# Splitting one more block product of a sequence-mixing matrix product, and reordering stores and gates around it

## The chip, the cores and the metric

The kernel runs on one core of one Trainium2 chip. The metric is the device time of one execution in microseconds (us), less is better. The core's engines run side by side, each with its own queue of instructions, in order: TensorE (PE, matrix products into PSUM banks), VectorE (DVE), ScalarE (ACT), GpSimd (POOL), and SyncE (SP), which here only issues DMAs.

## The reference

Two layers of two blocks each, on x of 2048 rows (S) by 512 columns (D), all in fp32:

```
x = x + A(layernorm(x))     # linear attention, 32 heads of 16
x = x + B(layernorm(x))     # gated MLP with mixing along the sequence
# and both once more

def B(x, w_in, w_sp, b_sp, w_out):
    z  = gelu(x @ w_in)                 # 2048 x 1792
    z1 = z[:, :896]
    z2 = layernorm(z[:, 896:])
    g  = w_sp @ z2 + b_sp[:, None]      # 2048 x 2048 times 2048 x 896: the mixing
    return (z1 * g) @ w_out
```

The weights are the same in both layers. The change concerns the mixing of layer two above all.

## The kernel before, in words

**Three products for one.** Every fp32 operand is split into a high part (ACT copies it to the format fp32r) and a low part (DVE subtracts the high part from the original). One fp32 product is then three matmuls: high x high, high x low, low x high. `high` (L222) and `low` (L225) are the helpers; the mixing has its own (L1777 and L1780 for blocks of w_sp, 128x1024; L1840, L1842 and L1844 for z2).

**Seven block products.** The mixing is cut into 2 x 2 blocks and done as seven block products instead of eight, with sums of blocks as operands (class `P4`; P1 to P7 in the order of `ORDER`: P2, P1, P6, P7, P4, P5, P3). The sums of w_sp's blocks (`Sums`) are made once, in layer one, kept in DRAM, and loaded again in layer two. The sums of z2's blocks are made in place in SBUF when a product needs them (`zsp`, operations on columns named H1, H2 and H3; "the H2 operations" are the subtraction and the addition that prepare columns H2). Products share PSUM banks: P6 goes on accumulating in P1's banks, and P7 in P6's.

**Two kinds of product.** An undivided product runs in eight steps along the contracted dimension: 24 matmuls of 128x512 a step where its `WITH3` columns are needed (P1, P2, P4, P5), 18 for the others (P6, P7, P3). A divided one (`DIVIDED`) is split into seven again, of half depth: fourteen steps of 12 matmuls (`mm_div`; the order of the seven is `SEVEN`, r = 1, 5, 6, 2, 7, 3, 4, two steps each, q = 0 and 1). Its operands are sums of quarter blocks of w_sp, which lie in DRAM (`halves`: a copy of one part, then an accumulating DMA from POOL's queue adds the other; `halve` does one of these each time it is called, from a list `parts`). After each pair of steps DVE adds the bank's content into units of the result (`evac_div`; a unit is 128 columns of the result over 512 rows, `unit(n, f)` in an SBUF tile `gb[n]`, called bg in the profile). Where the next product accumulates on, some columns are carried over into a bank by ACT (`carry`).

Before the change, layer one divides P2 and P4, layer two P2, P4 and P5.

**What a step needs.** Two steps ahead, `sp` prepares: the block of w_sp is loaded by SP (five steps ahead), ACT makes its high part, DVE its low part; for an undivided step DVE makes the sum of z2's blocks, ACT its high part, DVE its low part. `KEPT` products store their low parts of w_sp in layer one and load them in layer two by a DMA from POOL's queue (L1783), so that DVE doesn't make them again.

**Gates.** A finished unit is multiplied by z1, which comes from DRAM (`ask` loads up to three units of z1 ahead, in the order of `gates()`). One gate runs per step (`tick` of `P4`); those of P1's units on POOL (L2043), tied behind the latest high part of w_sp on ACT (`self.mark`). `evac` empties the banks of the undivided products on DVE (L2057 after P1, L2060 after P6).

**The rest.** Behind the mixing `out7` does the product with w_out and, in layer one, prepares layer two's attention. The order of all instructions is written out by hand: each engine's queue is what the code issues, in that order. The sums for the mixing are made in layer one beside the attention and the first product of block B: `Sums.tick` stores the last sums, fetches raw blocks and adds two of them on POOL. All pages (SBUF tiles of 128x512, `pg` in the profile) come from one pool of 22 and go round: a page that is put back is the next one's, as soon as the DMA that reads it has ended.

Of the kernel before, what the change touches and what calls it, by code (L numbers as in the profile page):

```python
# [15 lines left out]
P = 128  # L16
# [79 lines left out]
DIVIDED = ("P2", "P4"), ("P2", "P4", "P5")  # L96
KEPT = ("P7", "P5")
# [63 lines left out]
def mixer_kernel(ctx: ExitStack, tc: tile.TileContext, x_in, wqkv, wo_d, win1_d, win2_d, wsp_d, bsp_d, wout_d,  # L161
# [300 lines left out]
    class P1:  # L462
# [370 lines left out]
    class P2:  # L833
# [498 lines left out]
        def run(self, sums):  # L1332
# [4 lines left out]
            for s in range(1, NT + 3):  # L1337
# [3 lines left out]
                if s < 5:  # L1341
# [100 lines left out]
        def odd(self, s, p, q, r):  # L1442
# [168 lines left out]
    class Sums:  # L1611
# [3 lines left out]
        def __init__(self):  # L1615
# [13 lines left out]
            self.parts = [(what, p, m, q) for p in ("P4", "P5")[:len(DIVIDED[1]) - 1] for what in ("copy", "add") for m in (1, 3, 2, 4)  # L1629
                          for q in range(2)]  # L1630

# [6 lines left out]
        def halve(self, n, after, i=None):  # L1638
# [4 lines left out]
            row = 2 if p == "P2" else 0  # L1643
            j, s = {1: ((1, 0), (1, 4)), 3: ((0, 0), (1, 0)), 2: ((0, 0), None), 4: ((0, 4), None)}[m][what == "add"] or (0, 0)
            src = self.s1[j, s + 2 * q:s + 2 * q + 2] if p == "P5" else wsp_d[row + j, HT + s + 2 * q:HT + s + 2 * q + 2]
            if what == "copy":
                nc.sync.dma_start(self.halves[p, m, q], src)
            else:
# [6 lines left out]
                if after is not None:  # L1655
                    behind(d, after)

# [31 lines left out]
        def tick(self, ahead=True):  # L1689
# [5 lines left out]
            if ahead or self.todo[0][2] == 0:  # L1695
                self.fetch()
            k, j, h = self.todo.popleft()
# [12 lines left out]
    class P4:  # L1710
# [34 lines left out]
        def fetch1(self, g):  # L1745
            p, k = self.steps[g]
            t = self.halves.get()
            if p in self.div:
                r, q = self.SEVEN[k // 2], k % 2
                j, s = {1: (0, 0), 2: (0, 4), 4: (1, 4)}.get(r, (0, 0))  # L1750
                if r in (1, 2, 4):
                    s += 2 * q
                    ap = self.sums.s1[j, s:s + 2] if p == "P5" else wsp_d[(2 if p == "P2" else 0) + j, HT + s:HT + s + 2]
# [37 lines left out]
        def kept(self, g):  # L1791
            p, k = self.steps[g]
            if p not in KEPT or p == "P7" and k < 4:
                return None
# [10 lines left out]
        def zsp(self, g):  # L1805
# [13 lines left out]
            elif p == "P6":  # L1819
                z, sign = a[:, H2], -1.0  # L1820
# [29 lines left out]
        def zdiv(self, p, half, side, q, i):  # L1850
            return ztile[(0 if p == "P5" else HT) + 4 * half + 2 * q + i][:, 256 * side:256 * side + 256]
# [79 lines left out]
        def evac_div(self, p, r):  # L1931
# [4 lines left out]
            for f in range(2):  # L1936
# [6 lines left out]
                n, f = (2 + j if p == "P2" else j), 2 * half + f  # L1943
# [9 lines left out]
            if r in (2, 3, 4):  # L1953
                b = self.bank.pop(name)
                if p != "P5":
# [8 lines left out]
        def carry(self, j):  # L1964
# [3 lines left out]
            nc.scalar.activation(b, self.unit(j, 6), AF.Copy, scale=-1.0)  # L1968
# [77 lines left out]
        def evac(self, p, js=(0, 1)):  # L2046
# [3 lines left out]
            for j in js:  # L2050
                a, b = 2 + j, j
                for f in range(3):
# [3 lines left out]
                    elif p == "P1":  # L2056
                        V.tensor_add(self.unit(a, f), self.unit(a, f), q)  # L2057
                        gates.append((a, f))
                    elif p == "P6":
                        V.tensor_add(self.unit(a, 4 + f), q, bs[a])  # L2060
                    elif p == "P7":
                        V.tensor_sub(self.unit(b, 4 + f), bs[b], q)
# [418 lines left out]
```

## Time and profile before

| | |
|---|---|
| time, median of 3 runs | 1342.32 us (1341.86 to 1342.73) |
| the profiled execution's own time | 1342.64 us |
| its span | 1340.8 us |
| PE busy | 1333.3 us (99%) |
| DVE, ACT, POOL busy | 1056.3, 736.2, 461.8 us (79%, 55%, 34%) |
| DMA | 293.45 MB, mean 219 GB/s |
| layer two's mixing, P2 begins | 1009.20 us from the span's start |
| granted TensorE clock | full speed in all slices |

How to read it: the span is the time from the first to the last recorded instruction of one execution; the execution's own time is a little longer. "Busy" of PE is modelled, since matmuls overlap: one of 128x512 is recorded as 0.39 us long, though the next starts sooner. A row of a timeline reads: start, length, engine, line in the code, operation, output <- inputs, shape; in brackets, the idle time of that engine before it and what ended it.

### The profile page before, as it was taken

Reading aid. Unit: us, or ns where it says so; the run is one execution under the profiler, and the core shown is the slowest. Engines: PE = TensorE matmul, PEld = TensorE weight load, DVE = VectorE, ACT = ScalarE, POOL = GpSimd, SP = SyncE. Lnnn points to the kernel's source line nnn. Section 1 sums busy time; section 2 is a strip of 40 time slices with the busy share of each in tenths; the row PEclk is TensorE's granted clock in tenths of the full one; section 3 lists DMA queues with packets and bytes.
Section 4 is the critical chain, followed back from the end, with each engine's and each line's share of the span. In section 5 each row is a group of like instructions: output and inputs, shape, how many; then the busy total and the mean of one; then the engine's idle time right before and its main releaser. Section 6 shows DMA issues by size and latency. Waiting matters only on the chain.

```text
span 1340.8 us, 19229 instructions
## 1 busy us (share of the span) xinstructions
PE 1333.3 (99%) x6517; PEld 1136.2 (85%) x6517; DVE 1056.3 (79%) x1691; ACT 736.2 (55%) x1246; POOL 461.8 (34%) x611
## 2 busy tenths in 40 slices
PE   9999999999999999999999999999999999999998
PEld 7888788888888888889988888888888888888898
DVE  7679876567899789898866778777589758899885
ACT  5774544446742255345666655556687333666464
POOL 3765676433035400301422443545441022121021
PEclk9999999999999999999999999999999999999999
DMA  5898599887779986884864554788767555589344
GB/s 184 281 316 271 178 299 311 281 261 241 257 270 371 321 269 216 285 304 79 182 161 137 144 123 118 212 255 259 221 200 248 153 171 177 178 244 308 123 79 65
DMA packets 175283, 293.45 MB, mean 219 GB/s; under 512 B 14672, under 2 KB 55632, under 8 KB 174928
## 3 DMA queue, kind: packets, MB, share of 16 engines
q1 hardware_dynamic: 156064, 253.02, 57.2%
q0 software_dynamic: 18976, 39.07, 13.8%
q8 instruction: 51, 0.84, 0.3%
q14 instruction: 48, 0.39, 0.1%
q10 hardware_dynamic: 144, 0.13, 0.0%
HBM read 206.44 MB, written 102.50 MB: 230 GB/s over the span
## 4 chain that ended last, share of the span: by engine, by line
PE 93%; DVE 3%; DMA 3%; ACT 1%; POOL 0%; issue 0%; SPq 0%; DVEq 0%; ACTq 0%; POOLq 0%
PE bank L238 13%; PE bank L236 13%; PE bank L237 13%; PE bank L2002 11%; PE bank L2004 11%; PE bank L2003 11%; PE bank L2200 3%; PE bank L2201 3%; PE bank L2202 3%; PE bank L1163 1%; PE bank L1165 1%; PE bank L1164 1%; PE bank L992 1%; PE bank L994 1%; PE bank L993 1%; DMA qd<-s 1%
## 5 line engine op out<-in xcount | busy, mean ns | idle before, releaser
L2002 PE MATMUL bank<-qd,pg 128*128 128x512 f32 x736 | 286.6, 389 | 0.5 <-ACT pg L1840 0.3
L2004 PE MATMUL bank<-qd,pg 128*128 128x512 f32 x736 | 286.4, 389 | 0.0
L2003 PE MATMUL bank<-qd,pg 128*128 128x512 f32 x736 | 286.3, 389 | 0.0
L1777 ACT ACTIVATE qd<-qd 128x1024 fp32r<-128x1024 f32 x142 | 149.2, 1053 | 126.2 <-PE bank L2004 91.5
L1780 DVE TENSOR_TENSOR qd<-qd,qd 128x1024 fp32r<-128x1024 f32 x132 | 166.7, 1265 | 41.3 <-ACT qd L1777 41.1
L238 PE MATMUL bank<-qd,pg 128*128 128x512 f32 x448 | 174.8, 390 | 0.8 <-DVE pg L225 0.8
L2002 PEld LDWEIGHTS bank<-qd,pg 128*128 128x128 f32 x736 | 138.1, 188 | 29.9 <-ACT pg L1840 0.7
L2004 PEld LDWEIGHTS bank<-qd,pg 128*128 128x128 f32 x736 | 138.1, 188 | 28.9 <-DVE pg L1842 0.3
L2003 PEld LDWEIGHTS bank<-qd,pg 128*128 128x128 f32 x736 | 138.2, 188 | 28.7
L2043 POOL TENSOR_TENSOR bg<-bg,pg 128x512 f32<-128x512 f32 x28 | 48.4, 1730 | 188.4 <-ACT qd L1777 93.9
L236 PE MATMUL bank<-qd,pg 128*128 128x512 f32 x264 | 103.2, 391 | 0.2 <-ACT pg L222 0.2
L237 PE MATMUL bank<-qd,pg 128*128 128x512 f32 x264 | 102.9, 390 | 0.0
L238 PEld LDWEIGHTS bank<-qd,pg 128*128 128x128 f32 x448 | 84.1, 188 | 19.2 <-DVE pg L225 1.7
L1686 POOL TENSOR_TENSOR pg<-pg,pg 128x512 f32<-128x512 f32 x48 | 71.2, 1483 | 70.9 <-DMA pg<-in_wsp_dram 59.1
L2202 PE MATMUL bank<-wo,qd 128*128 128x256 f32 x288 | 81.5, 283 | 0.0
L371 POOL TENSOR_SCALAR rs<-mv 128x1 f32<-128x1 f32 x76 | 22.9, 302 | 166.1 <-DVE mv L369 154.9
L2200 PE MATMUL bank<-wo,qd 128*128 128x256 f32 x276 | 78.1, 283 | 0.0
L2201 PE MATMUL bank<-wo,qd 128*128 128x256 f32 x276 | 78.0, 283 | 0.0
L222 ACT ACTIVATE pg<-pg 128x512 fp32r<-128x512 f32 (+1 forms) x86 | 50.0, 592 | 44.3 <-DVE pg L1871 20.1
L225 DVE TENSOR_TENSOR pg<-pg,pg 128x512 fp32r<-128x512 f32 (+1 forms) x84 | 54.3, 656 | 9.6 <-ACT pg L222 9.2
L551 POOL TENSOR_TENSOR pg<-pg,pg 128x512 f32<-128x512 f32 x30 | 40.0, 1333 | 57.5 <-DVE pg L545 55.6
L236 PEld LDWEIGHTS bank<-qd,pg 128*128 128x128 f32 x264 | 49.6, 188 | 11.1 <-ACT pg L222 0.9
(299 smaller groups left out, 3342.2 us busy)
## 6 DMA issues: line engine op xcount, KB each, us to landing
qd<-s SPq DMA_DIRECT2D x62, 512.0 KB, 4.5
qd<-in_wsp_dram SPq DMA_DIRECT2D x40, 512.0 KB, 4.1
qd<-hP SPq DMA_DIRECT2D x40, 512.0 KB, 4.8
pg<-z SPq DMA_DIRECT2D x56, 256.0 KB, 4.7
pg<-in_wsp_dram SPq DMA_DIRECT2D x52, 256.0 KB, 4.9
s<-pg SPq DMA_DIRECT2D x48, 256.0 KB, 4.2
z<-pg SPq DMA_DIRECT2D x40, 256.0 KB, 3.6
pg<-w POOLq DMA_DIRECT2D x38, 256.0 KB, 5.2
```

Source lines behind the costliest of these rows:

```text
L236: nc.tensor.matmul(out, ah, bh, start=start, stop=False)
L237: nc.tensor.matmul(out, ah, bl, start=False, stop=False)
L238: nc.tensor.matmul(out, al, bh, start=False, stop=stop)
L1686: nc.gpsimd.tensor_tensor(t, a, b, op=OP.add)
L1777: self.mark = nc.scalar.activation(w[:, 0], r, AF.Copy)
L1780: nc.vector.tensor_sub(w[:, 1], r, w[:, 0].bitcast(F32))
L2002: m(out, h[:, o], w[:, 0, j, :], start=start, stop=False, skip_group_check=True)
L2003: m(out, h[:, o], w[:, 1, j, :], start=False, stop=False, skip_group_check=True)
L2004: m(out, l[:, o], w[:, 0, j, :], start=False, stop=stop, skip_group_check=True)
L2200: m(out, A, x, start=start and f == 0, stop=False, skip_group_check=True)
L2201: m(out, A, y, start=False, stop=False, skip_group_check=True)
L2202: m(out, B, x, start=False, stop=stop and f == 2, skip_group_check=True)
```

## The change

1. Layer two also divides P1. The eight copies of quarter blocks that this needs stand in layer one's `out7` (j = 0 and 1, four each, on SP), the eight additions, each in two halves, in layer two's attention (passes s = 1 to 16, on POOL).
2. P1 is a kept product in layer two. Its six low parts (r = 1, 2, 4, q = 0, 1) are made in layer two's attention, passes 1 to 7: one pass loads a block (`keepload`), the next splits it and stores the low part (`keep`). In layer two's mixing these six come by DMA.
3. The two H2 operations that P1's eight steps did on z2 go to P6's eight steps. Columns f = 2 of P1's result get a unit of their own (unit 6), which two additions on DVE join with unit 2 at P1's last step, two carries take to a bank for P6, and P6's f = 2 evictions and those of P2's new f = 2 units are done by ACT instead of DVE. Unit 6 of the other two tiles gets a sum of two biases in P6 (two additions on DVE), from which P7's f = 2 evictions subtract.
4. `sums.ask()` (stores and loads of the sums) is split from `Sums.tick` and called ahead of `a2` in layer one's first product of block B, for passes s < 5.
5. In `odd`, `self.raw(0)` stands behind `q()`.
6. z1 is loaded in the order in which the gates use it.

The diff, cut to its core:

```diff
-DIVIDED = ("P2", "P4"), ("P2", "P4", "P5")
-KEPT = ("P7", "P5")
+DIVIDED = ("P2", "P4"), ("P2", "P1", "P4", "P5")
+KEPT = ("P7", "P5", "P1")
+KEEP = 1
...
                 if self.L:
+                    sums.keep()
+                    if s >= KEEP:
+                        sums.keepload()
+                    if s <= NT:
+                        sums.halve(40 + (s - 1) // 2, None, (s - 1) % 2)
...
                     self.c3(s - 1)
+                    sums.ask()
                     self.a2(s + 2)
                     self.p1.late_phi_a()
                     self.a(s + 3)
-                    sums.tick()
+                    sums.tick(ask=False)
...
+                q()
                 self.raw(0)
-                q()
                 self.first_a(2)
...
+        def keepload(self):
+
+            if self.unkept:
+                j, s = self.unkept.popleft()
+                t = quads.get([P, 2, 2, 512])
+                nc.sync.dma_start(t[:, 0], wsp_d[2 + j, s:s + 2].rearrange("j p t -> p j t"))
+                self.split = t, self.lows["P1"][j, s:s + 2].rearrange("j p t -> p j t")
+
+        def keep(self):
+
+            if self.split is not None:
+                (t, at), self.split = self.split, None
+                r, h = t[:, 0], t[:, 1].bitcast(F32R)
+                high(h, r)
+                low(r.bitcast(F32R), r, h)
+                nc.sync.dma_start(at, r)
+                quads.put(t)
...
             elif p == "P6":
+                if "P1" in self.div:
+                    nc.vector.tensor_sub(a[:, H2], a[:, H1], a[:, H2])
+                    nc.vector.tensor_add(a[:, H2], a[:, H2], b[:, H2])
                 z, sign = a[:, H2], -1.0
...
+                if p == "P1" and f == 2:
+                    f = 6
+                elif p == "P1":
+                    new = False
+                elif p == "P2" and f == 2 and new and "P1" in self.div:
+                    nc.scalar.activation(self.unit(n, f), bank, AF.Copy, scale=float(sign))
+                    continue
...
-            return ([(2 + j, 3) for j in js] + [(2 + j, f) for j in js for f in range(3)]
+            return ([(2 + j, f) for j in js for f in range(3)] + [(2 + j, 3) for j in js]
...
+                    elif p == "P6" and f == 2 and "P1" in self.div:
+                        nc.scalar.activation(self.unit(a, 6), q, AF.Copy)
...
+                    for k in range(4 if j < 2 else 0):
+                        self.sums.halve(32 + 4 * j + k, None)
...
+                    if p == "P1":
+                        if k == 10:
+                            self.ask(3)
+                        if k > 10 and k < 13:
+                            self.carry(p, 12 - k)
+                        if k == 13:
+                            for j in range(2):
+                                nc.vector.tensor_add(self.unit(2 + j, 2), self.unit(2 + j, 2), self.unit(2 + j, 6))
+                            self.gq.extend([(2 + j, f) for j in range(2) for f in range(3)] + [(2 + j, 3) for j in range(2)])
...
+                if p == "P6" and k in (2, 3) and "P1" in self.div:
+                    nc.vector.tensor_add(self.unit(k - 2, 6), self.bs[k - 2], self.bs[k])
```

Three places show what this moves in the queues. First DVE, from the last steps of layer two's P1 into P6, before: L1780 is the low part of a block of w_sp, L1817 and L1818 are P1's two H2 operations, L1842 and L1844 low parts of z2, L2057 and L2079 the evictions of P1's banks.

```order
L1780 TENSOR_TENSOR qd_149_11022<-qd_126_10264,qd_149_11022 128x1024
L1817 TENSOR_TENSOR z_z_9305<-z_z_9305 128x384
L1818 TENSOR_TENSOR z_z_9305<-z_z_9305,z_z_10168 128x384
L1842 TENSOR_TENSOR pg_1025_11028<-z_z_9305,pg_1024_11027 128x512
L1780 TENSOR_TENSOR qd_150_11056<-qd_127_10394,qd_150_11056 128x1024
L1844 SCALAR_TENSOR_TENSOR pg_1027_11060<-z_z_8593,pg_1026_11059 128x384
L1780 TENSOR_TENSOR qd_151_11094<-qd_127_10394,qd_151_11094 128x1024
L1844 SCALAR_TENSOR_TENSOR pg_1032_11098<-z_z_8686,pg_1031_11097 128x384
L2057 TENSOR_TENSOR bg_27_10528<-bg_27_10528,bank_381_10855 128x512
```

And after: L1996 are evictions of P1's block products (r = 3, then r = 4), L1814 is the low part of a block of w_sp, L1855 and L1856 are the H2 operations, L1881 the low part of z2, L2438 the join of units 2 and 6.

```order
L1996 TENSOR_TENSOR bg_27_10591<-bg_27_10591,bank_384_10983 128x512
L1814 TENSOR_TENSOR qd_162_11203<-qd_132_10327,qd_162_11203 128x1024
L1855 TENSOR_TENSOR z_z_8656<-z_z_8656 128x384
L1856 TENSOR_TENSOR z_z_8656<-z_z_8656,z_z_9620 128x384
L1881 SCALAR_TENSOR_TENSOR pg_1048_11209<-z_z_8656,pg_1047_11208 128x384
L1814 TENSOR_TENSOR qd_163_11227<-qd_132_10327,qd_163_11227 128x1024
L1855 TENSOR_TENSOR z_z_8749<-z_z_8749 128x384
L1856 TENSOR_TENSOR z_z_8749<-z_z_8749,z_z_9621 128x384
L1881 SCALAR_TENSOR_TENSOR pg_1050_11233<-z_z_8749,pg_1049_11232 128x384
L1996 TENSOR_TENSOR bg_28_10592<-bg_28_10592,bank_381_10968 128x512
L1996 TENSOR_TENSOR bg_28_10592<-bg_28_10592,bank_382_10969 128x512
L2438 TENSOR_TENSOR bg_27_10591<-bg_27_10591 128x512
```

P6's first two steps are prepared ahead of the last eviction in both, and now carry two more operations each. Second, SP in layer one's first product of block B, before: L428 stores a transposed tile (qt), L1681 stores two sums (s), L204 loads.

```order
L919 DMA x_0_79<-pg_170_1518 128x512
L428 DMA qt_3_1749<-pg_188_1673 128x4x128
L1681 DMA s_145<-pg_175_1542 128x512
L1681 DMA s_2_131<-pg_174_1540 128x512
L204 DMA pg_196_1758<-in_wsp_dram 128x512
L204 DMA pg_197_1760<-in_wsp_dram 128x512
```

And after, where the same are L429, L1707 and L205:

```order
L925 DMA x_0_79<-pg_170_1527 128x512
L1707 DMA s_145<-pg_175_1551 128x512
L1707 DMA s_2_131<-pg_174_1549 128x512
L205 DMA pg_195_1755<-in_wsp_dram 128x512
L205 DMA pg_196_1757<-in_wsp_dram 128x512
L429 DMA qt_3_1766<-pg_188_1682 128x4x128
```

The stores of the sums and the loads now stand ahead of the store of qt. Third, DVE at layer two's first product of block B, before: L1170 is `raw(0)`, L443 copies a bank to z_y, L225 makes a low part.

```order
L457 STREAM_TRANSPOSE z_y<-pg_939_10008 128x4x128
L225 TENSOR_TENSOR qd_123_9904<-z_y,qd_122_9903 128x4x128
L1170 TENSOR_TENSOR qd_124_10124<-qd_120_9389,qd_121_9390 128x1024
L443 COPY z_y<-bank_359_10126 128x512
L225 TENSOR_TENSOR qd_123_9904<-z_y,qd_122_9903 128x4x128
```

And after, as L1176, L444 and L226:

```order
L458 STREAM_TRANSPOSE z_y<-pg_939_10071 128x4x128
L226 TENSOR_TENSOR qd_129_9967<-z_y,qd_128_9966 128x4x128
L444 COPY z_y<-bank_359_10188 128x512
L226 TENSOR_TENSOR qd_129_9967<-z_y,qd_128_9966 128x4x128
L1176 TENSOR_TENSOR qd_130_10187<-qd_126_9452,qd_127_9453 128x1024
```

`raw(0)` now stands behind the copy and its low part. On PE nothing is moved; 24 matmuls of P1 are gone.

More of the change, by code (lines that the diff above doesn't have):

```diff
@@ L1628, in __init__ @@
                         self.halves[p, m, q] = dram.tile([2, P, 512], F32, name=f"h{p}_{m}_{q}")
-            self.parts = [(what, p, m, q) for p in ("P4", "P5")[:len(DIVIDED[1]) - 1] for what in ("copy", "add") for m in (1, 3, 2, 4)
+            self.parts = [(what, p, m, q) for p in ("P4", "P5", "P1") for what in ("copy", "add") for m in (1, 3, 2, 4)
                           for q in range(2)]
+            self.unkept, self.split = deque((j, s + 2 * q) for j, s in ((0, 0), (0, 4), (1, 4)) for q in range(2)), None
         def fetch(self):
@@ L1687, in add, with ask @@
             self.made.append((m, k, j, t))
-        def tick(self, ahead=True):
+        def ask(self, ahead=True):
             self.store()
@@ L1696, in tick @@
                 self.fetch()
+        def tick(self, ahead=True, ask=True):
+            if ask:
+                self.ask(ahead)
+            if not self.todo:
+                return
             k, j, h = self.todo.popleft()
@@ L1792, in kept @@
             p, k = self.steps[g]
-            if p not in KEPT or p == "P7" and k < 4:
+            if p not in KEPT or p == "P7" and k < 4 or p == "P1" and not self.L:
                 return None
@@ L1850, in zdiv @@
         def zdiv(self, p, half, side, q, i):
-            return ztile[(0 if p == "P5" else HT) + 4 * half + 2 * q + i][:, 256 * side:256 * side + 256]
+            return ztile[(0 if p in ("P1", "P5") else HT) + 4 * half + 2 * q + i][:, 256 * side:256 * side + 256]
         def zsum(self, g):
@@ L2061, in evac @@
                     elif p == "P7":
-                        V.tensor_sub(self.unit(b, 4 + f), bs[b], q)
+                        own = f == 2 and "P1" in self.div
+                        V.tensor_sub(self.unit(b, 4 + f), self.unit(b, 6) if own else bs[b], q)
                         if "P4" in self.div:
```

20 lines of the change are left out of this document (12 added, 8 removed).

## The prediction

> **What bounds the kernel now.** I read the page's busy times first, then its chain, then the waits of TensorE (PE) in both halves of the span, then timelines around the places that the change touches. All times are us. The busy row:
>
> ```profile
> PE 1333.3 (99%) x6517; PEld 1136.2 (85%) x6517; DVE 1056.3 (79%) x1691; ACT 736.2 (55%) x1246; POOL 461.8 (34%) x611
> PE 93%; DVE 3%; DMA 3%; ACT 1%; POOL 0%; issue 0%; SPq 0%; DVEq 0%; ACTq 0%; POOLq 0%
> ```
>
> PE carries 93% of the chain. Busy alone would not prove that a matmul less is time less, since the records overlap; so here are starts at the head of layer two's mixing (start, busy, line):
>
> ```profile
> 1009.20 0.39 PE L2002 MATMUL bank<-qd,pg 128*128 128x512 f32 x1
> 1009.42 0.39 PE L2003 MATMUL bank<-qd,pg 128*128 128x512 f32 x1
> ...
> 1011.92 0.39 PE L2002 MATMUL bank<-qd,pg 128*128 128x512 f32 x1
> ```
>
> 1009.20 to 1011.92 is a step of twelve, so a matmul costs 2.72 / 12 = 0.2267. A step of a divided product is 2.72; a step of P6 or P7 (18 matmuls) is 18 x 0.2267 = 4.08. What PE still waits for, after the start-up (total, times, longest):
>
> ```profile
> PE bank L238 <- DVE pg L225: 0.8, 1, 0.8
> PE bank L2002 <- ACT pg L1840: 0.3, 1, 0.3
> ...
> PE bank L1163 <- ACT bank L1180: 0.4, 1, 0.4
> PE bank L2002 <- DVE bg L1952: 0.2, 1, 0.2
> ```
>
> So PE is at its own pace nearly everywhere; a matmul removed is worth its whole start interval, as long as VectorE (DVE) and ScalarE (ACT) bring its operands in time.
>
> **The change, part by part.**
>
> *Fewer matmuls.* Layer two's P1 goes from 8 steps of 24 to 14 of 12: 192 - 168 = 24 fewer, and PE's order shows nothing else. 24 x 0.2267 = **-5.44**. A page of the Trainium skill, "Perfetto Trace Analysis" (section "Identifying the Most-Contended Engine"), says that matmul busy time is a poor measure of distance to the limit and that the share of weight loading should be taken; by that, with PEld at 85%, the gain would be 85% of 5.44, 4.6, and the forecast 0.8 higher. The trace disagrees for this purpose: the starts above are evenly spaced with no hole, so I price by starts.
>
> *P1's own stage.* Two windows (PE, PEld, DVE, ACT, POOL busy, clock, DMA share, GB/s): P1 as it is, and P5, which is divided already and takes kept low parts:
>
> ```profile
> 1047.00:1091.00 44.00, 44.00 (x195) 36.43 (x195) 26.12 (x39) 12.32 (x17) 1.29 (x1) 1.00 0.43 133
> 1194.00:1232.00 38.00, 38.00 (x169) 31.47 (x168) 36.18 (x58) 23.55 (x38) 11.13 (x10) 1.00 0.96 316
> ```
>
> A divided product fills DVE to 36 of 38 and PE still does not wait inside P5. P1 has P5's form without the work on w_out, and six of its fourteen low parts come by DMA. I put nothing here; the kept low parts are the slow rival below.
>
> *P1 to P6.* Here is the same seam in the old kernel, P5 to P3 (DVE, then ACT, then PE):
>
> ```profile
> 1229.53 1.28 DVE L1952 TENSOR_TENSOR bg<-bg,bank 128x512 f32<-128x512 f32 x2
> 1230.72 1.22 DVE L1780 TENSOR_TENSOR qd<-qd,qd 128x1024 fp32r<-128x1024 f32 x1
> 1231.86 0.55 DVE L1842 TENSOR_TENSOR pg<-z_z,pg 128x384 fp32r<-128x384 f32 x1
> 1232.33 1.22 DVE L1780 TENSOR_TENSOR qd<-qd,qd 128x1024 fp32r<-128x1024 f32 x1
> 1233.46 0.55 DVE L1842 TENSOR_TENSOR pg<-z_z,pg 128x384 fp32r<-128x384 f32 x1
> 1233.93 1.28 DVE L1952 TENSOR_TENSOR bg<-bg,bank 128x512 f32<-128x512 f32 x2
> ```
>
> ```profile
> 1230.36 0.58 ACT L1968 ACTIVATE bank<-bg 128x512 f32<-128x512 f32 x1
> 1230.88 1.04 ACT L1777 ACTIVATE qd<-qd 128x1024 fp32r<-128x1024 f32 x1
> 1231.83 0.51 ACT L1840 ACTIVATE pg<-z_z 128x384 fp32r<-128x384 f32 x1
> ```
>
> ```profile
> 1234.05 0.39 PE L2004 MATMUL bank<-qd,pg 128*128 128x512 f32 x1
> 1234.67 0.50 PE L2002 MATMUL bank<-qd,pg 128*128 128x512 f32 x1 [0.23 <-DVE bg L1952]
> ```
>
> DVE prepares two steps ahead (L1780, L1842 twice) and only then empties the banks of the last block product (r = 4), which the tenth matmul of the next product needs. PE starts 0.62 apart there instead of 0.23: listed 0.23, lost 0.39 and another 0.11 in the slow restart (0.50 against 0.39 busy). Start to start the prices are: eviction pair 1.19, W's low part 1.14, z's low part 0.47; on ACT a carry 0.52, W's high part 0.95, z's high part ending 0.51 after its start.
>
> After the change P1 hands over to P6 in this order, but each P6 step also has two H2 operations, moved out of P1. Their price, and what a gate on GpSimd (POOL) does to them, stands in P6 and P7 of the old kernel (DVE, POOL, ACT):
>
> ```profile
> 1112.49 1.23 DVE L1780 TENSOR_TENSOR qd<-qd,qd 128x1024 fp32r<-128x1024 f32 x1 [1.29 <-ACT qd L1777]
> 1113.63 1.64 DVE L1827 TENSOR_TENSOR pg<-z_z 128x384 f32<-128x384 f32 x1
> 1115.31 0.56 DVE L1829 TENSOR_TENSOR z_z<-z_z,z_z 128x384 f32<-128x384 f32 x1
> 1115.79 0.55 DVE L1831 TENSOR_TENSOR z_z<-z_z,z_z 128x384 f32<-128x384 f32 x1
> ```
>
> ```profile
> 1112.54 2.32 POOL L2043 TENSOR_TENSOR bg<-bg,pg 128x512 f32<-128x512 f32 x1 [1.75 <-ACT qd L1777]
> 1116.91 1.29 POOL L2043 TENSOR_TENSOR bg<-bg,pg 128x512 f32<-128x512 f32 x1 [2.05 <-ACT qd L1777]
> ```
>
> ```profile
> 1111.40 1.06 ACT L1777 ACTIVATE qd<-qd 128x1024 fp32r<-128x1024 f32 x1 [2.61 <-PE bank L2004]
> 1115.36 0.53 ACT L1840 ACTIVATE pg<-pg 128x384 fp32r<-128x384 f32 x1 [2.90 <-DVE pg L1827]
> 1115.79 1.04 ACT L1777 ACTIVATE qd<-qd 128x1024 fp32r<-128x1024 f32 x1
> ```
>
> An H2 operation alone costs 0.48 (1115.31 to 1115.79). Count from P6's first matmul as zero. r = 3's banks are full two steps earlier, at -5.44; the pair takes 1.19 (-4.25); W's low part 1.14 and two H2 operations 0.96 (-2.15); ACT's z high part 0.51 (-1.6). Behind it on ACT stand a carry 0.52 and W's high part 1.04 (0.0), then DVE again: 1.14 + 0.96 (2.1), z high 0.51 (2.6), z low 0.47 (3.1), and half of r = 4's eviction, 0.6 (3.7). PE reaches that bank after nine matmuls, 2.04. **+1.7**.
>
> *Inside P6.* Before, DVE sat idle in each P6 step until ACT had split W. Now there is a ring: DVE's low part, two H2 operations, ACT's z high part, ACT's next W high part. Old P7 shows it with one H2 operation ahead of ACT, with a gate beside it: from L1777's end at 1112.46 to the next end at 1116.83 is 4.37. The gate is tied to that same L1777, starts with DVE's low part, and the operation behind the low part takes 1.64 instead of 0.56: 1.08 lost. With the second H2 operation the ring is 4.37 + 0.48 = 4.85 beside a gate, 0.77 over PE's 4.08, and 3.77 without, below it. The eight gates of P1's units come one in each P6 step, as before; five of them stand beside steps 3 to 7. Step 2 is ready at 3.1 + 1.2 (eviction) + 1.2 (two adds of P1's units, taken at an eviction's price) + 1.14 + 0.96 + 0.51 + 0.47 = 8.6, PE needs it at 1.7 + 8.16 = 9.9: slack 1.3. 5 x 0.77 - 1.3 = **+2.5**.
>
> The Trainium skill's "SBUF — State Buffer" (section "Who interferes with whom") says that a DVE instruction with two SBUF inputs contends with a GpSimd instruction that reads SBUF, the one that starts first holding the port for all of its time. The trace agrees (1.64 beside 0.56), and by that rule a gate could take its whole 1.29 from the ring: 5 x 0.2 = 1.0 more than I sum, 1341.6.
>
> *P6 to P7.* P7's first step needs the banks of P6 emptied, which stands on DVE behind the preparation of that step. Step 7 ready means z's low part just done; W's low part follows 0.6 later, then 1.14, an H2 operation beside the eighth gate 1.64, two more 0.96, a short one 0.2, z low 0.47, half an eviction 0.6: 5.6 after step 7 begins, PE wants it at 4.08. +1.5, and some 0.4 more in P7's second step, whose preparation stands behind four evictions (from nothing to 0.8): **+1.9**.
>
> New waits: 1.7 + 2.5 + 1.9 = **+6.1**. If two of the five gates find DVE waiting anyway it is 1.5 less, 4.6; with no slack at step 2 and 0.8 in P7's second step it is 7.8.
>
> *The reorders.* Three of the waits listed above are addressed. The rows (DVE, SP, DVE, DVE):
>
> ```profile
> 155.68 0.69 DVE L225 TENSOR_TENSOR pg<-bank,pg 128x512 fp32r<-128x512 f32 x1 [2.15 <-DMA s<-pg]
> ```
>
> ```profile
> 151.47 0.38 SPq L428 DMA_DIRECT2D qt<-pg  x1
> 151.94 0.94 SPq L1681 DMA_DIRECT2D s<-pg  x2
> ```
>
> ```profile
> 454.79 4.54 DVE L1842 TENSOR_TENSOR pg<-pg,pg 128x384 fp32r<-128x384 f32 x1
> ```
>
> ```profile
> 972.96 1.22 DVE L1170 TENSOR_TENSOR qd<-qd,qd 128x1024 f32<-128x1024 f32 x1
> ```
>
> First, DVE's L225 waits 2.15 for a page whose store (L1681) stood behind the store L428 on SP; asked earlier, it goes first. Second, in layer one the gates came in a bunch, because z1 was loaded in another order than gated, and held DVE 4.54 at L1842; L1840's wait is behind that. Third, L1170 stood ahead of the copy that L1180 needs. Each listed wait costs about 0.3 beyond its figure, by the seam above (0.23 listed, 0.50 lost): 0.8 + 0.3, 0.3 + 0.3, 0.4 + 0.3 = **-2.4**; nothing, if something else is late just behind, and no more than 2.7.
>
> *Covered, at nothing.* Layer two's first half gets, in seven passes, six loads, splits (1.04 on ACT, 1.14 on DVE) and stores, and sixteen small accumulating DMAs from POOL. The window there:
>
> ```profile
> 700.00:740.00 40.00, 40.00 (x179) 33.10 (x178) 27.57 (x47) 27.09 (x44) 13.19 (x23) 1.00 0.41 125
> ```
>
> DVE and ACT have 12 and 13 of 40 free and PE does not wait; six splits take 7 and 6 over some 50. If the loads came late, ACT would stand at the split with the pass's other work behind it; that cover gone, the six splits cost their 7. The eight block copies at the end of layer one stand on SP behind what the last product loads; no PE wait there is due to DMA.
>
> **Sum.** -5.44 + 6.1 - 2.4 = -1.7. The profiled execution took 1342.64 (its span of 1340.8 and 1.84 around it), so 1340.9; the median of three runs is 0.32 lower: **1340.6**.
>
> **Rivals.** *A, the ring keeps up.* If the gates run where DVE waits anyway (they start when ACT's part ends, and a z1 load can hold them), the ring is 3.77 and only the first seam and a late half eviction at P7, 0.5, remain: -5.44 + 2.2 - 2.4 = -5.6, 1336.7; without the seam either, -7.8, 1334.5. For it: 3.77 is below 4.08. Against: row 1113.63. *B, slower: kept low parts late.* The six loads of low parts go out on POOL's queue when the buffer of the step four back is free: three steps, 8.16, before their step, and the second matmul of each group uses them a little later. Above about 10 from release to landing, each step waits. At 11, 1.0 in each of six steps: 1340.6 + 6 = 1346.6. For it: one more transfer per step in a queue that is first used in P1. Against: P5 takes the same at a DMA share of 0.96 without a listed wait, and P1's share is 0.43. *C, the reorders give nothing* because the next thing is late by as much: -5.44 + 6.1 = +0.7, 1343.0. That the division is not executed cannot be: PE's order has the 24 fewer.
>
> **Chances.** About 0.2% (2.7) is what a measurement of this kernel tells from no change. My forecast with its spread (waits 4.6 to 7.8, reorders 2.7 to 1.2: -3.5 to +1.2, 1338.8 to 1343.5), within which C lies: 0.55, a fifth of it beyond 2.7 faster. A: 0.36, all faster. B and unseen costs of the first half: 0.09, of which one in nine stays within 2.7. Faster 0.11 + 0.36 = 0.47, same 0.44 + 0.01 = 0.45, slower 0.08. The range leaves out B, and of A the end below 1335.5 (no seam at all): 1335.5 to 1343.6. The likeliest case's own range is 1338.8 to 1343.5.
>
> **What would show it.** P1 in 38.1 of PE's time without waits; a wait on the eviction of r = 4 (the successor of L1952) at the tenth matmul of P6, 1.4 or more; waits of P6's steps 4 to 7 for DVE or ACT, with the operation behind W's low part at 1.6 beside each gate; a late first bank in P7; the three old waits gone. It is wrong if P6 runs in 32.7 (A), if PE in P1 waits for DMA (B), or if the old waits stand where they were (C).

## The result and the profile after

The changed kernel takes 1353.35 us (median of 6 runs, 1350.96 to 1355.19) against 1342.43 before (6 runs): slower by 0.8%, ratio 1.0083 with a 95% interval of 1.0072 to 1.0094. The forecast was 1340.6 with a range up to 1343.6. The profiled execution took 1353.23 us, 10.6 more than the one before.

Busy times and chain of the profile after (us, share of the span):

```profile
PE 1333.4 (99%) x6493; PEld 1131.2 (84%) x6493; DVE 1073.5 (79%) x1729; ACT 757.0 (56%) x1278; POOL 480.1 (36%) x633
PE 84%; DVE 6%; DMA 5%; ACT 2%; issue 1%; SPq 1%; POOL 1%; ACTq 0%; POOLq 0%; DVEq 0%
```

PE reads as busy as before, with 24 matmuls fewer, in a span 10.6 longer: its busy time hides the loss. The chain shows it: PE's share went from 93% to 84%, DVE's and DMA's from 3% each to 6% and 5%. The waits of PE, first half of the span and second half (total, times, longest; in the first half the start-up's and two of 0.2 are left out):

```profile
PE bank L239 <- DVE qd L226: 1.0, 1, 1.0
PE bank L237 <- ACT qd L223: 0.9, 1, 0.9
```

```profile
PE bank L237 <- DVE pg L226: 6.3, 4, 1.8
PE bank L2049 <- ACT pg L1877: 1.7, 4, 0.5
PE bank L2049 <- DVE bg L2109: 1.6, 1, 1.6
PE bank L2049 <- DVE bg L1996: 0.8, 1, 0.8
PE bank L1952 <- DMA qd<-lowP: 0.5, 1, 0.5
PE bank L2051 <- DVE pg L1879: 0.2, 1, 0.2
```

Adding 0.3 for each listed wait, as in the prediction: the first row of the second half, 7.5 us, lies at 712 to 752 us, in layer two's attention, where I had put nothing. L1996, L1877, L2109 and L1879 are the seam P1 to P6, the ring in P6 and the start of P7: 1.1 + 2.9 + 1.9 + 0.5 = 6.4, where I had put 6.1. A kept low part cost 0.8 in P1. The two rows of layer one (320 and 232 us) are new; the old waits at 156, 465 and 976 us are gone. -5.44 + 7.5 + 6.4 + 0.8 = +9.3, most of the 10.6.

The starts of PE's matmuls close the sum. Outside layer two's P1 both kernels issue the same matmuls in the same order; how much later the same matmul starts after the change, at the ends of each stretch, tells what the stretch lost:

| stretch of PE's order | lost, us | forecast |
|---|---|---|
| up to layer one's first product of block B | -0.17 | 0 |
| layer one's first product of block B (156, 232, 320 us) | +1.95 | -1.1 |
| layer one's mixing (465 us) | -0.39 | -0.6 |
| layer two's attention | +7.54 | 0 |
| layer two's first product of block B (976 us) | -0.37 | -0.7 |
| P1 (24 matmuls fewer, one low part late) | -4.62 | -5.44 |
| P1 to P6 | +1.05 | +1.7 |
| inside P6 | +3.60 | +2.5 |
| start of P7 | +2.41 | +1.9 |
| P5 to P3 | -0.36 | 0 |
| sum | +10.6 | -1.7 |

Where the text below says "by the starts", it is this reading, against the kernel before.

**The attention.** The chain that ended last runs through it thus (start, length, what):

```profile
698.50 1.24 DVE qd L226
699.75 0.37 SPq L1681
700.17 0.46 SPq L1671
...
702.74 6.87 DMA pg<-xt
709.66 0.60 issue
710.26 1.21 DVE qd L226
711.49 0.37 SPq L1681
...
714.47 5.25 DMA pg<-xt
719.77 0.60 issue
720.37 1.21 DVE qd L226
721.60 0.37 SPq L1681
```

DVE makes the kept low part (L226, 128x1024); SP stands at its store (L1681) until then; only behind it come the next pass's loads, the transposed tile `xt` among them; DVE must transpose that tile before it gets to the next kept low part; PE waits for what DVE does behind that:

```profile
709.63 0.73 DVE L458 STREAM_TRANSPOSE bank<-pg 128x512 f32<-128x512 f32 x1 [3.45 <-DMA pg<-xt]
```

```profile
712.91 0.50 PE L237 MATMUL bank<-qd,pg 128*128 128x512 f32 x1 [1.32 <-DVE pg L226]
```

One turn takes 11.7 and 10.1 us (699.75 to 711.49 to 721.60). A pass took 8.16 before, by the same transpose there:

```profile
710.08 0.72 DVE L457 STREAM_TRANSPOSE bank<-pg 128x512 f32<-128x512 f32 x1
718.24 0.72 DVE L457 STREAM_TRANSPOSE bank<-pg 128x512 f32<-128x512 f32 x1
```

The transposes of 700 to 760 us, before and after (busy, mean ns, idle before them):

```profile
L457 DVE STREAM_TRANSPOSE bank<-pg 128x512 f32<-128x512 f32 x8 | 5.7, 716 | 0.0
```

```profile
L458 DVE STREAM_TRANSPOSE bank<-pg 128x512 f32<-128x512 f32 x7 | 5.1, 723 | 9.2 <-DMA pg<-xt 9.2
```

Before, DVE never waited for that load; after, it waits 9.2 in the same stretch, and makes seven passes instead of eight.

**P1 to P7.** DVE, then PE, at the seam; the successors of the rows of P5 to P3:

```profile
1087.98 1.37 DVE L1996 TENSOR_TENSOR bg<-bg,bank 128x512 f32<-128x512 f32 x2 [3.80 <-PE bank L2051]
...
1096.96 1.28 DVE L1996 TENSOR_TENSOR bg<-bg,bank 128x512 f32<-128x512 f32 x2
```

```profile
1093.69 0.73 PE L1952 MATMUL bank<-qd,pg 128*128 128x512 f32 x2 [0.53 <-DMA qd<-lowP]
...
1097.70 0.50 PE L2049 MATMUL bank<-qd,pg 128*128 128x512 f32 x1 [0.77 <-DVE bg L1996]
```

And the ring in P6, DVE and then POOL's gates (L2090):

```profile
1103.67 1.23 DVE L1814 TENSOR_TENSOR qd<-qd,qd 128x1024 fp32r<-128x1024 f32 x1 [0.39 <-ACT qd L1811]
1104.81 1.64 DVE L1855 TENSOR_TENSOR z_z<-z_z 128x384 f32<-128x384 f32 x1
...
1108.59 1.23 DVE L1814 TENSOR_TENSOR qd<-qd,qd 128x1024 fp32r<-128x1024 f32 x1 [0.39 <-ACT qd L1811]
...
1113.64 2.31 DVE L1814 TENSOR_TENSOR qd<-qd,qd 128x1024 fp32r<-128x1024 f32 x1
```

```profile
1103.71 2.33 POOL L2090 TENSOR_TENSOR bg<-bg,pg 128x512 f32<-128x512 f32 x1 [4.94 <-ACT qd L1811]
...
1113.55 1.31 POOL L2090 TENSOR_TENSOR bg<-bg,pg 128x512 f32<-128x512 f32 x1 [2.59 <-ACT qd L1811]
```

A turn of the ring is 4.92 (1103.67 to 1108.59), then 5.05, beside PE's 4.08; the prediction had 4.85. The two turns of 5.05 also hold the additions of biases (0.68 each, at 1113.04 and 1118.08), for which its sum had no row. At 1103.71 DVE was first, and the operation behind its low part took 1.64; at 1113.55 the gate was first, and the low part itself took 2.31 instead of 1.23.

### The profile page after: what moved, and what is told of

It is laid out like the page before. It is cut to its first block, busy times and chain, and to the rows that moved or that the text cites. A ratio compares the mean times of both kernels' runs of the same rounds, so it can differ in the third digit from the quotient of the medians.

```text
span 1351.4 us, 19331 instructions
## 1 busy us (share of the span) xinstructions
PE 1333.4 (99%) x6493; PEld 1131.2 (84%) x6493; DVE 1073.5 (79%) x1729; ACT 757.0 (56%) x1278; POOL 480.1 (36%) x633
## 4 chain that ended last, share of the span: by engine, by line
PE 84%; DVE 6%; DMA 5%; ACT 2%; issue 1%; SPq 1%; POOL 1%; ACTq 0%; POOLq 0%; DVEq 0%
PE bank L2051 11%; PE bank L2049 11%; PE bank L2050 11%; PE bank L239 10%; PE bank L237 10%; PE bank L238 10%; PE bank L2250 3%; PE bank L2251 3%; PE bank L2252 3%; DMA pg<-xt 2%; DMA yt<-z_y 1%; PE bank L1169 1%; PE bank L1171 1%; PE bank L1170 1%; PE bank L998 1%
## 5 line engine op out<-in xcount | busy, mean ns | idle before, releaser
L2049 PE MATMUL bank<-qd,pg 128*128 128x512 f32 x704 | 274.8, 390 | 4.1 <-ACT pg L1877 1.7
L2051 PE MATMUL bank<-qd,pg 128*128 128x512 f32 x704 | 274.6, 390 | 0.2 <-DVE pg L1879 0.2
L2050 PE MATMUL bank<-qd,pg 128*128 128x512 f32 x704 | 274.0, 389 | 0.0
L1811 ACT ACTIVATE qd<-qd 128x1024 fp32r<-128x1024 f32 x148 | 155.5, 1052 | 87.6 <-PE bank L2051 41.1
L1814 DVE TENSOR_TENSOR qd<-qd,qd 128x1024 fp32r<-128x1024 f32 x132 | 169.5, 1286 | 29.5 <-ACT qd L1811 29.3
L239 PE MATMUL bank<-qd,pg 128*128 128x512 f32 x448 | 174.7, 390 | 0.0
L2049 PEld LDWEIGHTS bank<-qd,pg 128*128 128x128 f32 x704 | 132.1, 188 | 34.0 <-ACT pg L1877 3.7
L2051 PEld LDWEIGHTS bank<-qd,pg 128*128 128x128 f32 x704 | 132.1, 188 | 29.5 <-DVE pg L1881 1.3
L2050 PEld LDWEIGHTS bank<-qd,pg 128*128 128x128 f32 x704 | 132.1, 188 | 27.3
L237 PE MATMUL bank<-qd,pg 128*128 128x512 f32 x264 | 103.5, 392 | 6.5 <-DVE pg L226 6.3
L238 PE MATMUL bank<-qd,pg 128*128 128x512 f32 x264 | 103.0, 390 | 0.0
L239 PEld LDWEIGHTS bank<-qd,pg 128*128 128x128 f32 x448 | 84.1, 188 | 18.0 <-DVE pg L226 0.4
L1712 POOL TENSOR_TENSOR pg<-pg,pg 128x512 f32<-128x512 f32 x48 | 69.7, 1453 | 71.6 <-DVE pg L1879 51.5
L2090 POOL TENSOR_TENSOR bg<-bg,pg 128x512 f32<-128x512 f32 x28 | 49.4, 1767 | 127.0 <-ACT qd L1811 120.7
L223 ACT ACTIVATE pg<-pg 128x512 fp32r<-128x512 f32 (+1 forms) x94 | 55.2, 595 | 51.3 <-DVE pg L1908 21.0
L458 DVE STREAM_TRANSPOSE bank<-pg 128x512 f32<-128x512 f32 x58 | 41.5, 716 | 35.6 <-DMA pg<-yt 21.7
L237 PEld LDWEIGHTS bank<-qd,pg 128*128 128x128 f32 x264 | 49.6, 188 | 18.5 <-DVE pg L226 8.1
L226 DVE TENSOR_TENSOR pg<-pg,pg 128x512 fp32r<-128x512 f32 (+1 forms) x92 | 59.7, 658 | 6.2 <-ACT pg L223 5.7
```

The source lines that it names most:

```text
L237: nc.tensor.matmul(out, ah, bh, start=start, stop=False)
L238: nc.tensor.matmul(out, ah, bl, start=False, stop=False)
L239: nc.tensor.matmul(out, al, bh, start=False, stop=stop)
L1712: nc.gpsimd.tensor_tensor(t, a, b, op=OP.add)
L1811: self.mark = nc.scalar.activation(w[:, 0], r, AF.Copy)
L1814: nc.vector.tensor_sub(w[:, 1], r, w[:, 0].bitcast(F32))
```

## The experiments

All are compared with the kernel before in the same series; its medians there were 1341.9 to 1342.2, against 1342.43 in the changed kernel's own series. So a difference from the changed kernel's 1353.35 is uncertain by some 0.5 for that alone.

**The reorders alone** (the kernel before, with three edits):

```diff
+                    sums.ask()
                     self.a2(s + 2)
...
-                    sums.tick()
+                    sums.tick(ask=False)
...
+                q()
                 self.raw(0)
-                q()
...
+            return ([(2 + j, f) for j in js for f in range(3)] + [(2 + j, 3) for j in js]
```

> The kernel before with the reorders alone: ask() ahead of a2, q() ahead of raw(0), z1 in the order of the gates. Theory (asking earlier puts SP's loads of qt behind the sums and sets the whole ring of layer one's first product 2 us late, which PE meets later): the waits at 156, 465 and 976 us go (1.25, 0.4, 0.4), new ones of 1.4 at 232 and 1.7 at 317 to 320 come; +0.5 to +1.5 over the kernel before, 1343 to 1344. Rival, the prediction's term: -2.4, 1340.0. Rival, the new waits at 232 and 320 come from other traffic of the change: they are absent here.

Measured: 1342.04, ratio 0.9998 (0.9989 to 1.0007), so between -1.5 and +0.9 us. The new one among PE's waits in the first half of its span:

```profile
PE bank L238 <- DVE qd L225: 1.0, 1, 1.0
```

That is the wait at 319 us. The waits at 156, 465 and 976 us are gone, and this one is there without any of the change's other traffic. By the starts, the places at 465 and 976 us gained 0.7 and 0.35, and layer one's first product lost 0.7. The prediction's -2.4 falls; so does my +0.5 to +1.5. The wait at 232 us did not show here: how large the new waits are differs from profile to profile.

**Stores a pass later** (the changed kernel):

```diff
+            if self.kst is not None:
+                t, at = self.kst
+                nc.sync.dma_start(at, t[:, 0])
+                quads.put(t)
+                self.kst = None
             if self.split is not None:
-                (t, at), self.split = self.split, None
-                r, h = t[:, 0], t[:, 1].bitcast(F32R)
+                self.kst, self.split = self.split, None
+                t = self.kst[0]
+                r, h = t[:, 0], t[:, 1].bitcast(F32R)
                 high(h, r)
                 low(r.bitcast(F32R), r, h)
-                nc.sync.dma_start(at, r)
-                quads.put(t)
```

> The changed kernel with the store of each of the six kept low parts one pass later, so that SP doesn't wait for DVE ahead of the next pass's loads. Theory (SP stands at that store, a ring low part - store - load of the transposed tile - transpose - low part of about 10 us beside PE's 8.16): the four waits of 7.4 us in all at 712 to 752 us go, 1346, and the runs scatter less. Rival (the added DMA traffic or the added work of ACT and DVE is what PE waits for): 1351 to 1355 as it is.

Measured: 1350.28 (1349.89 to 1353.01), ratio 1.0071 (1.0057 to 1.0085). Two of the four waits are left, 3.0 instead of 6.3:

```profile
PE bank L237 <- DVE pg L226: 3.0, 2, 1.9
```

SP's queue shows why (then the chain's piece between the two):

```profile
710.98 0.52 SPq L1679 DMA_DIRECT2D lowP<-qd  x1
717.77 0.37 SPq L1672 DMA_DIRECT2D qd<-in_wsp_dram  x1
```

```profile
710.98 6.77 DMA lowP<-qd
```

Only two buffers are free in this stage. With a store one pass later, the next load takes the very buffer that is being stored, and SP stands 6.8 us at that load (L1672) instead of at the store. The theory was half tested: the place where SP stands had moved.

**Three buffers in turn** (the two free buffers hold two halves each; three halves go round, the fourth holds the high part):

```diff
+                    self.room = [quads.get([P, 2, 2, 512]) for _ in range(2)]
+                    a, b = self.room
+                    self.ring, self.temp = deque((a[:, 0], a[:, 1], b[:, 0])), b[:, 1]
                 j, s = self.unkept.popleft()
-                t = quads.get([P, 2, 2, 512])
-                nc.sync.dma_start(t[:, 0], wsp_d[2 + j, s:s + 2].rearrange("j p t -> p j t"))
+                t = self.ring.popleft()
+                nc.sync.dma_start(t, wsp_d[2 + j, s:s + 2].rearrange("j p t -> p j t"))
...
+            if self.kst is not None:
+                t, at = self.kst
+                nc.sync.dma_start(at, t)
+                self.ring.append(t)
```

> The changed kernel with three buffers in turn for the kept low parts: a store goes out one pass after its split, and a load takes a buffer whose store went out a pass before, so that SP stands at neither. Theory (SP's standing, at the store in the changed kernel and at the load in the one with late stores, is what makes PE wait in layer two's attention): its waits go, -7 to -9, 1344.5 to 1346.5. Rival (added traffic and work of ACT and DVE): the waits stay above 4.

Measured: 1346.23, ratio 1.0029 (1.0018 to 1.0040): 7.1 less than the changed kernel's 1353.35. All of PE's waits in layer two's attention and its first product:

```profile
PE bank L237 <- DVE pg L226: 0.2, 1, 0.2
```

The same loads, splits and stores, with the same bytes and the same work on ACT and DVE, cost almost nothing once SP stands at none of them (0.5 by the starts, against 7.5). The rival of traffic and work falls.

**No kept low parts for P1:**

```diff
-KEPT = ("P7", "P5", "P1")
+KEPT = ("P7", "P5")
...
-                    sums.keep()
-                    if s >= KEEP:
-                        sums.keepload()
```

> The changed kernel without kept low parts for P1: no loads, splits and stores in layer two's attention, DVE makes all fourteen low parts of P1. Theory: -7.4 in the attention, -0.8 at P1's last kept low part, and at most +4 in P1, where DVE gets 6 x 1.14 = 6.8 us more work beside about 33 of 38: 1346 to 1350. Rival (P1 would be bound by DVE without kept parts): P1 over 42 us, 1350 or more.

Measured: 1344.07 (1342.91 to 1346.71), ratio 1.0019 (1.0010 to 1.0028): 9.3 less than the changed kernel, and less than the 1346 to 1350 that I expected. P1 with all fourteen low parts on DVE (window; PE, PEld, DVE, ACT, POOL busy, clock, DMA share, GB/s):

```profile
1045.00:1087.00 42.00, 42.00 (x187) 34.80 (x186) 38.52 (x62) 23.30 (x35) 0.00 (x0) 1.00 0.69 218
```

DVE is busy 38.5 of 42 and PE does not wait in it: the 4 that I had allowed for did not come, and by the starts P1 gains its full 5.44. The kept low parts of P1 bought nothing.

**`ask()` undone in the changed kernel:**

```diff
-                    sums.ask()
                     self.a2(s + 2)
...
-                    sums.tick(ask=False)
+                    sums.tick()
```

> The changed kernel with ask() undone. Theory (the earlier ask costs 3.2 in layer one's first product and brings 1.25): -2, 1351.4, with the wait at 156 us back and those at 232 and 317 to 320 gone. Rival, the prediction's term: +1.1, 1354.5.

Measured: 1353.32, ratio 1.0085 (1.0071 to 1.0099): no difference that these runs can tell. The profile has the wait at 156 us back and none at 232 and 320, as expected. But by the starts the attention lost 2.2 more than in the changed kernel's profile, as much as the expected gain. Its waits are only 0.6 longer there (6.9 in all); most of the rest are eight matmuls behind the last of them that start 0.43 apart instead of 0.23, while the granted clock is down to 0.50 (the column behind POOL):

```profile
751.00:753.00 2.00, 2.00 (x6) 1.54 (x6) 0.85 (x2) 2.00 (x4) 1.23 (x2) 0.50 0.11 36
```

So this pair of runs does not price `ask()`.

**Eviction first:**

```diff
-                div_first = p in self.div and k == 13 and p == "P4"
+                div_first = p in self.div and k == 13 and p in ("P4", "P1")
```

> The changed kernel with the eviction of P1's last block product ahead of the preparation of P6's second step. Theory: the wait at P6's tenth matmul (0.9 to 1.8) goes, and step 1 comes at most 0.5 late instead; the ring with the gates still loses as much per step and eats the rest, so -0.5 to -1.5 in P6, in a total of 1352 to 1353. Rival (the eviction isn't what PE waits for): no change in P6.

Measured: 1354.05, ratio 1.0082 (1.0069 to 1.0095): no gain. The waits from P6 to P7 show where it went:

```profile
PE bank L2049 <- ACT pg L1877: 3.3, 6, 1.1
PE bank L2049 <- DVE bg L2109: 1.6, 1, 1.6
```

The wait for the eviction is gone, and the wait for z's high part behind the ring is 3.3 in six places instead of 1.7 in four. While the ring is slower than PE, what is saved ahead of it is given back in it: by the starts 0 at the seam instead of 1.05, and 6.3 inside P6 instead of 3.6.

**Gates on DVE** (P1's eight gates in layer two):

```diff
-            if f > 2 and (n < 2 or f > 3):
+            if f > 2 and (n < 2 or f > 3) or self.L and n > 1 and f < 4:
                 nc.vector.tensor_mul(u, u, z1)
```

> The changed kernel with the eight gates of P1's units on DVE instead of POOL, behind z's low part, where DVE waits for ACT. Theory (a gate on POOL holds the operation behind W's low part for 1.1, a gate on DVE costs 0.6 that the ring has free): the waits of P6's steps 4 to 7 (3.2) go, and P7's first two (2.4) fall to 1 or less; -4 to -5, 1348.5 to 1349.5. Rival (the ring is too slow by itself with two more H2 operations): eight times 0.6 more on DVE make P6 longer, 1354 to 1357.

Measured: 1348.81, ratio 1.0052 (1.0037 to 1.0066): 4.5 less. By the starts, nothing is lost inside P6 instead of 3.6, 1.2 at the start of P7 instead of 2.4, and 1.9 at the seam instead of 1.1, so 3.9 less in all; this profile's other differences (3.1 less in layer one's first product, 2.6 more in the attention) lie where the edit changes nothing. DVE in P6, with the gate as L2088:

```profile
1098.94 1.22 DVE L1814 TENSOR_TENSOR qd<-qd,qd 128x1024 fp32r<-128x1024 f32 x1
1100.08 0.55 DVE L1855 TENSOR_TENSOR z_z<-z_z 128x384 f32<-128x384 f32 x1
...
1102.29 0.68 DVE L2088 TENSOR_TENSOR bg<-bg,pg 128x512 f32<-128x512 f32 x1
1102.89 1.22 DVE L1814 TENSOR_TENSOR qd<-qd,qd 128x1024 fp32r<-128x1024 f32 x1
```

L1855 takes 0.55 again, and a turn takes 3.95 (1098.94 to 1102.89) with the gate in it, below 4.08. No wait for L1877 is left in P6. The rival, that the ring is too slow by itself, falls. One DVE operation more made DVE faster. A page of the Trainium skill, "SBUF — State Buffer" (section "Who interferes with whom"), has this rule: a DVE instruction with two SBUF inputs and a GpSimd instruction that reads SBUF exclude each other, and the first holds the port to its end. All three cases of P6 agree: 1.64 behind a low part that came first, 2.31 for one that came second, and 0.55 without a gate.

**The three together** (buffers in turn, eviction first, gates on DVE; the edits above):

> The three together: buffers in turn, eviction first, gates on DVE. If the three costs are separate: -8 - 1 - 4.5, about 1340; -5.44 and nothing lost would be 1337.

Measured: 1340.03, ratio 0.9980 (0.9971 to 0.9990): faster than the kernel before. The single savings are 7.1 and 4.5, and nothing for the eviction; together it is 13.3, since the eviction pays once the ring keeps up: by the starts the seam costs 1.9 with the buffers alone and with the gates alone, and 0 here. In the second half of the span two waits are left, both at the start of P7:

```profile
PE bank L2060 <- DVE bg L2120: 1.2, 1, 1.2
PE bank L2062 <- DVE pg L1890: 0.2, 1, 0.2
```

**The same without kept low parts** (no kept parts, eviction first, gates on DVE):

> The changed kernel without kept low parts for P1, with the eviction first and the gates on DVE. If P1 has room for the six low parts on DVE, as it looked without kept parts: the same as with buffers in turn and all three, 1339.5 to 1340.5. Rival (kept parts are worth their loop): 2 or more above it, 1342.

Measured: 1340.15, ratio 0.9982 (0.9973 to 0.9990), as with the buffers in turn.

**The additions of biases in P1:**

```diff
-                if p == "P6" and k in (2, 3) and "P1" in self.div:
-                    nc.vector.tensor_add(self.unit(k - 2, 6), self.bs[k - 2], self.bs[k])
...
                     if p == "P1":
+                        if k in (6, 7):
+                            nc.vector.tensor_add(self.unit(k - 6, 6), self.bs[k - 6], self.bs[k - 4])
```

> As the one before, with the two additions of biases (0.6 each on DVE) in P1's steps 6 and 7 instead of P6's 2 and 3, where the ring has no room. Theory: of the wait at P7's first step (1.3) the 1.2 that was late goes, 1338.5 to 1339.5. Rival (P7 waits for its own preparation): no change.

Measured: 1338.50 (1336.70 to 1340.14), ratio 0.9965 (0.9952 to 0.9977): 1.65 less. By the starts, P6 and the start of P7 lose 1.8 instead of 3.0 in the profile of the one before: the expected 1.2. P7's first step waits 0.7 instead of 1.2; the rest was spread over P6, in delays too small for the list. What remains of the 1.65 is no more than the scatter.

**The same additions, with buffers in turn:**

> Buffers in turn, eviction first, gates on DVE, and the two additions in P1's steps 6 and 7: within 0.7 of the one before if kept parts neither help nor cost.

Measured: 1340.55, ratio 0.9992 (0.9983 to 1.0001): 2.0 above the one before, where at most 0.7 was expected. The profiled executions differ by that too (1338.77 against 1336.70), but their waits in layer two are alike; by the starts 2.3 of the difference is layer one's first product, with two waits at 232 and 320 us, which no kept part touches. Over the profiles of all kernels with the earlier `ask()` that product comes out between 1.4 shorter and 2.0 longer than before, with the same code there. So the miss is most likely that place's. That this is so in the unprofiled runs, where the two intervals do not overlap, is not shown.

**`ask()` undone there** (no kept parts, eviction first, gates on DVE, additions in P1):

> The one with the additions in P1 and no kept parts, with ask() undone. Theory (asking earlier moves the wait at 156 us to 232 and 317 to 320 and neither gains nor loses beyond the scatter): within 0.7 of it, the wait of 1.2 at 156 back, the scatter between runs smaller. Rival, the prediction's term: 1.1 slower.

Measured: 1337.89 (1337.80 to 1338.11), ratio 0.9962 (0.9950 to 0.9974): within 0.7 of it, with five runs inside 0.3 us. The wait at 156 us is back, and in the second half of the span P7's start is what is left:

```profile
PE bank L239 <- DVE pg L226: 1.0, 1, 1.0
```

```profile
PE bank L2045 <- ACT bg L2103: 0.7, 1, 0.7
PE bank L2047 <- DVE pg L1875: 0.2, 1, 0.2
```

This has the lowest median of all, 4.3 us less than the kernel before (1342.16 in this series). The profile with `ask()` earlier (1336.70) has neither this wait nor the new ones: in that execution the prediction's term came true, while its other runs took up to 1340.14. That the five runs here lie so close is no proof that `ask()` makes the others scatter: the kernel before has no earlier `ask()` either, and its runs in this series went from 1340.77 to 1345.95.

## Why the prediction was wrong, point by point

- **Fewer matmuls, -5.44.** Right. By the starts P1 is 5.44 shorter wherever it does not wait, as without kept parts and in the fastest kernel, and not the 4.6 of the pricing by weight loading. With the new waits taken away, the whole change made the kernel 4.3 us faster than before (1342.16 to 1337.89), with 1.8 still lost in P6 and P7.
- **P1's own stage, nothing.** Nearly right. Rival B's mechanism came once: P1's last kept low part was issued at 1083.49 and used at 1093.69, 10.2 later, and cost 0.8.

```profile
1083.49 0.71 POOL L1817 DMA_DIRECT2D qd<-lowP  x1 [2.02 <-PE bank L2051]
```

- **P1 to P6, +1.7; inside P6, +2.5; P6 to P7, +1.9.** Right in place and cause: 1.1, 3.6 and 2.4 by the starts, 7.1 against 6.1. The first is smaller because PE was 0.8 late already; where it was not, it is 1.9. The second is larger because a turn takes 4.9 to 5.05, not 4.85. A gate held DVE for 1.1, as summed, and not for its whole 1.29. The gates on DVE show that the collision is the cause in P6. Rival A, that the ring keeps up, fails.
- **The reorders, -2.4.** Wrong. Each of the three named waits went, but the whole is 0 (-1.5 to +0.9). By the starts the second and third bring 0.4 to 0.7 and 0.35 in nearly every profile. The first brings its 1.4 in some executions, and in others loses up to 3.3 again, 76 to 164 us later in the same product. The prediction kept as lower end "nothing, if something else is late just behind"; that was rival C, and it is so for the first. Why asking earlier makes SP's later loads late I followed only along the chain of one profile; no run separates it further.
- **"Covered, at nothing."** This is the step that failed, by 7.5 us. (The block copies at layer one's end and the small accumulations were covered: no wait of PE is new there, and without kept parts the attention lost nothing.) I weighed the attention's additions by the free time of ACT and DVE, and gave the stores no price. The split and the store of a kept part also tie two queues together: SP stands at the store until DVE has come to the low part, with the next pass's loads queued behind it, and DVE needs one of these to come to the next low part. Whether ACT or DVE has room does not enter into it. I named what would queue on ACT if a load came late, and not what queues on SP while it waits for DVE; that one row was missing from the sum. That the 7 I named for late loads is near the 7.5 is luck: it is the splits' own work, and the same splits lost 0.5 with three buffers in turn.

The forecast would have been 1348.1 with that term (1340.6 + 7.5). The table says where the other 5.2 of the 1353.35 are: the reorders lost 1.2 in that profile instead of bringing 2.4 (3.6), the waits from P1 to P7 were 1.0 larger, P1's kept part cost 0.8, and 0.5 came back at P5 to P3 and ahead of layer one's first product. The rest, 0.4, is the difference between the medians and the profiled executions.

## What to carry to other kernels

A store that is issued on a queue in order is a wait for its producer, and everything behind it on that queue waits too: when work is added "beside" a loop, follow each added DMA on its queue, ask which engine it waits for, and whether that engine needs something that is queued behind it. A ring of that kind has a period of its own (11.7 and 10.1 us here, beside a loop of 8.16); once the slack ahead of it is used up it costs its excess, however idle the engines look. And where VectorE is on the critical ring, an operation on GpSimd beside it may cost more than the same operation on VectorE.

## What was not expected of the hardware

A gate of 1.3 us on POOL held DVE for 1.1 whichever of the two began first: 1.64 instead of 0.55 for the operation behind, or 2.31 instead of 1.23 for the one that came second. The same gate on DVE took 0.6 from start to start. And PE's recorded busy time was 99% in both profiles, with 7.5 us of waits in one stage alone: the chain and the waits showed it, the busy time did not.

In three of the profiled executions (stores a pass later, `ask()` undone, gates on DVE) the granted clock fell to 0.50 behind the last wait of layer two's attention (1.9, 2.0 and 2.6 us long), and eight matmuls started 0.43 apart instead of 0.23: some 1.6 us lost behind the wait itself. In the changed kernel's profile (1.75) and with the eviction first (2.2) it did not fall. No run here shows what decides it.
